# First 1024 tokens' attention by pairs of heads instead of by 128 tokens, in an attention and two-MLP kernel on one core

## The chip, the cores and the metric

The kernel runs on one core of a Trainium2 chip. The metric is the device time of one execution in microseconds (us); lower is better. Engines are named as in the profile: PE (matrix products), PEld (its loads of the stationary operand), DVE (vector), ACT (scalar), POOL, and SP, which issues the DMAs.

## The reference

Chunked attention, then two gated MLPs over the same 4608 tokens (8 batches of 576 tokens, 8 heads of 64).

```python
B, H, S, D = 8, 8, 576, 64                  # q, k, v
q_c, k_c, v_c = (t.reshape(B, H, 9, 64, D) for t in (q, k, v))
scores = matmul(q_c, k_c^T) / sqrt(D)       # 64 x 64 in each chunk
attn = softmax(scores)
x = matmul(attn, v_c)                       # to [4608 tokens, 512]
g = x @ w_gate                              # 512 -> 1536
x = (g * sigmoid(g) * (x @ w_val)) @ w_out  # 1536 -> 512
xn = x / sqrt(mean(x*x) + 1e-6) * rms_g
out = the same gated MLP on xn with the second set of weights
```

The MLP weights arrive as 64-bit floats; the kernel loads them as pairs of 32-bit words and makes a high and a low part of each on the chip.

## The kernel before, in words

The tokens are cut into 9 blocks of 512 (j), a block into 4 tiles of 128 tokens (i = 0 to 35; a tile is two chunks). The hidden width is cut into 12 pieces of 128 (f). The first MLP runs per block j and piece f: `emit_g` (12 products: 4 pieces of the contraction, each as high x high, low x high, high x low), `emit_v` (12 more), and `emit_y` of the piece before (12). `mm3` issues the three products (L493 to L495). The second MLP follows, with a seven-product scheme that the change does not touch.

The order of all instructions is written out by hand. The table `at` holds small steps (attention of the next block, loads, weight preparation) that run at set places between `emit_g`, `emit_v` and `emit_y`; `put(l, j, pos, fn)` enters one, and three positions make one f.

Ahead of the loop stands a start written out step by step, the attention of tiles 0 to 3, that is of the first block. Per tile:

- `load_tok` (L305): q and k of 128 tokens and all 8 heads, one DMA each, in pieces of 64 floats;
- `trans_tok` (L312, copies L321): 4 + 4 PE transposes of 128 x 128, one per pair of heads, and two ACT copies into `qT`, `kT`;
- `att_s` (L355): 16 score products of 64 x 64;
- `att_m` (L374, L375, L381): maximum and subtraction on DVE, exponential on ACT;
- `att_n` (L388 to L393): sum and reciprocal on DVE, product on POOL;
- `att_t` (L417, L424): 4 PE transposes and a copy to `pT`;
- `att_pv` (L451): 16 products with `xv`; the cast of the result to `xh` on ACT (L469) and the rest, `xl`, on DVE (L487, `att_lo`).

Tiles 4 to 7 (the second block) take the same steps from the table, between the products of block 0. Tiles from 8 on use `trans_att` and `att_both`, and are left alone.

The first MLP's weights are prepared in the list order `w1` = g0, v0, o0, g1, v1, o1, ... (piece number behind the letter), three DVE and three ACT operations each: `rebase` (ACT L112, L116), `to_f32` (DVE L131, L136), the cast to the high part (ACT L152), `to_lo` (DVE L159). `conv1(z)` does one step of that for three weights at once; `pre_w1` issues their loads (512 KB each, L101).

PSUM has the pairs of banks `a` and `yb` (two banks each) and the banks `g`, `v`, `y0`, `y1`.

Of the kernel before, what the change touches and what calls it, by code (L numbers as in the profile page):

```python
# [9 lines left out]
F32 = mybir.dt.float32  # L10
# [9 lines left out]
def tile_kernel(  # L20
# [192 lines left out]
    groups = [list(range(0, 2 * EARLY - 2)), list(range(2 * EARLY - 2, 2 * EARLY))]  # L213
# [37 lines left out]
    def load_v(g):  # L251
        if g == 0:
            two = [spare_tile([P, 2, HP, D], f"xv_0_{n}") for n in range(len(groups[0]) // 2)]
            gt.setdefault(g, [None] * 3)[2] = lambda z, hp, n, hpar: two[n // 2][z:z + 64, hpar, hp, :]
            dmas = []
            for n, t in enumerate(two):
                s = n * P
                for hpar, z, c, w in ((0, 0, 0, P), (1, 64, 0, CH), (1, 0, CH, CH)):
                    dmas.append((
                        t[z:z + w, hpar],  # L260
                        v[0, hpar::2, s + c:s + c + w, :].rearrange("h p d -> p h d"),
                    ))
            return dmas
# [21 lines left out]

    def load_tok(i):
        ts_ = []
        dmas = []
        for nm, src in (("q", q), ("k", k)):
            if i < EARLY:  # L290
                t = spare_tile([P, H, D], f"t{nm}{i}")
            else:
                z, f = again.pop(0)
                t = wraw.tile([P, H, D], F32, tag=f"w{z}{f}", name=f"t{nm}{i}")
# [6 lines left out]
    def trans_tok(i, tags=None):  # L301
        ts_ = []
        both = ps_pair("a", f"qkP{i}") if tags is None else None
        pts = []
        for z, nm in enumerate("qk"):  # L305
            t = tok[i][z]
            if both is None:
                pt = ps.tile([P, HP, P], F32, tag=tags[z], name=f"{nm}P{i}")
            else:
                pt = both[:, z].rearrange("p (h q) -> p h q", h=HP)  # L310
# [4 lines left out]
            pts.append(pt)  # L315
        for z, nm in enumerate("qk"):
            if i < NW // P:
                sb = spare_tile([P, HP, P], f"{nm}T{i}")
            else:
                sb = att.tile([P, HP, P], F32, tag=f"{nm}T", name=f"{nm}T{i}")  # L320
            nc.scalar.copy(sb, pts[z])  # L321
            ts_.append([sb[:, hp] for hp in range(HP)])
        qkT[i] = ts_
# [23 lines left out]
    def att_s(i, tag="a", sb=None):  # L347
        qT, kT = qkT.pop(i)
        if sb is None:
            sb = ps_pair(tag, f"s_{i}")[:, :, :HP * CH]  # L350
# [89 lines left out]
    def att_pv(i, j, tag="a", xb=None, put_off=False):  # L440
        pT = probT.pop(i)
        if xb is None:
            xb = ps_pair(tag, f"xb_{i}")[:, :, :HP * CH]
        xb = xb.rearrange("p c (h q) -> p c h q", h=HP)
        for hp in range(HP):
            for c in range(2):
                g, n = where[2 * i + c]
                vt = gt[g][2]
                for hpar in range(2):
                    z = (hpar ^ c) * 64  # L450
                    nc.tensor.matmul(  # L451
                        xb[hpar * 64:hpar * 64 + 64, c, hp, :],
                        vt(z, hp, n, hpar),
                        pT[z:z + 64, hp, c * 64:c * 64 + 64],
                        start=True,
                        stop=True,
                    )
        xh, xl = x_tiles(0, j)
        o = i * P - blocks[j][0]
# [4 lines left out]

    def att_hi(i, j):
        xb = xps[i]
        xh, xl = x_tiles(0, j)
        o = i * P - blocks[j][0]
        nc.scalar.copy(xh[:, :, o:o + P].rearrange("p h (c q) -> p c h q", c=2), xb)  # L469
# [12 lines left out]
    def att_lo(i, j):  # L482
        xb = xps.pop(i)
        xh, xl = x_tiles(0, j)
        o = i * P - blocks[j][0]
        ah, al = (t[:, :, o:o + P].rearrange("p h (c q) -> p c h q", c=2) for t in (xh, xl))
# [9 lines left out]

    def emit_g(l, j, f):
# [3 lines left out]
        g = ps.tile([P, 512], F32, tag="g", name=f"g{l}_{j}_{f}")  # L501
        for c in range(KD):
# [157 lines left out]
    for x, (l, j) in enumerate(seq):  # L660
        if x + 1 < len(seq):
            nl, nj = seq[x + 1]
            if nl == 0:
                for n, i in enumerate(tiles_of(nj)):
# [13 lines left out]
                    else:  # L678
                        b = (0, 9, 18, 27)[n]
                        late = n == 0  # L680
                        put(l, j, b + (2, 1, 0, 0)[n], lambda i=i: trans_tok(i))
                        put(l, j, b + 2 + late, lambda i=i: att_s(i))
# [5 lines left out]
                    for c in (2 * i, 2 * i + 1):  # L688
                        g = where[c][0]
                        if g > 0 and c == groups[g][-1] and g + 2 < len(groups):  # L690
                            dq, dv, nq = {4: (21, 18, 10), 7: (3, 9, 12), 8: (8, 12, 12)}.get(i, (1, 11, 8))
# [14 lines left out]
    spread(0, 0, 4, 10, lambda: load_v(2))  # L706
# [298 lines left out]
    with tc.manual_schedule():  # L1005
        nc.vector.memset(ones.bitcast(F32), 1.0)
        make_identity(nc, ident)
        w1 = [(nm, f) for f in range(NF) for nm in "gvo"]
        loaded = 0
# [33 lines left out]

        NI = NW // P
        issue(load_tok(0))
        issue(load_tok(1))
        issue(load_tok(2))
        issue(load_tok(3))
        first_v = load_v(0)
        issue(first_v[:3])  # L1050
        pre_w1(1)
        issue(first_v[3:])
# [3 lines left out]
        later = load_v(1)  # L1056
        sb_ = ("a", "yb")
        xb_ = (("g", "v"), ("y0", "y1"))
        trans_tok(0, xb_[0])
        trans_tok(1, xb_[1])  # L1060
        att_s(0, sb_[0])
        att_m(0)
        trans_tok(2, xb_[0])
        att_s(1, sb_[1])
        att_m(1)
        trans_tok(3, xb_[1])
        att_n(0)
        att_s(2, sb_[0])
        att_m(2)
        att_n(1)  # L1070
        att_s(3, sb_[1])
        att_t(0, xb_[0][0])
        rebase(0, *w1[0])
        att_m(3)
        att_n(2)
        att_t(1, xb_[1][0])
        att_n(3)
        att_pv(0, 0, "a")
        att_pv(1, 0, "yb")
        att_lo(0, 0)  # L1080
        att_lo(1, 0)
        att_t(2, xb_[0][1])
        att_t(3, xb_[1][1])
        to_f32(0, *w1[0], cast=False)
        att_pv(2, 0, "a")
        cast_hi(*w1[0])
        att_pv(3, 0, "yb")
        att_lo(2, 0)
        to_lo(*w1[0])
        att_lo(3, 0)  # L1090
        rebase(0, *w1[1])
        conv1(1)
# [188 lines left out]
```

## Time and profile before

| | us |
|---|---|
| median of 3 runs (1751.49 to 1754.25) | 1751.93 |
| profiled execution, its own time | 1752.0 |
| its span | 1750.2 |
| PE busy (10086 matmuls) | 1732.6, 99% of the span |
| DVE busy | 1262.3, 72% |
| ACT busy | 674.4, 39% |
| POOL busy | 393.4, 22% |
| DMA: 379.73 MB, mean | 217 GB/s |

Busy time is the union of an engine's instructions. "Idle before" names what ended an engine's wait. In lists in order of time a group of equal instructions is one line with its count. A product of full 32-bit floats (scores, and the products with `xv`) is recorded as two matmuls, so 16 score products show as x32; a transpose, and a product of the MLP, is recorded as one. Matmuls overlap, so the time from one start to the next is what one costs, and the duration beside it is longer.

### The profile page before, as it was taken

The numbers are of one execution on the slowest core, as the hardware profiler recorded it, in microseconds if no ns is written. First come the engines' busy times: TensorE is split into PE (matmuls) and PEld (weight loads), VectorE is DVE, ScalarE is ACT, GpSimd is POOL, SyncE is SP. The second block draws the span as 40 slices with busy tenths as digits, with TensorE's granted clock in tenths as the row PEclk, the third lists the DMA queues.
The fourth block names the chain that finished last, engine by engine and source line by source line (L and its number), as shares of the span: only waits on it lengthen the run. The fifth ranks groups of instructions, "written<-read, shape, count | busy, mean of one in ns | idle before, by whom it ended". The sixth has DMA issues, their size and how long they took to land.

```text
span 1750.2 us, 28897 instructions
## 1 busy us (share of the span) xinstructions
PE 1732.6 (99%) x10086; PEld 1468.3 (84%) x10086; DVE 1262.3 (72%) x2250; ACT 674.4 (39%) x1248; POOL 393.4 (22%) x391
## 2 busy tenths in 40 slices
PE   7999999999999999999999999999999999999998
PEld 5788888888888888888888888888888888999998
DVE  6986887888878788876536567944794488568566
ACT  6872333233332422332122434523453354345343
POOL 1002244244423524341121211200110011002000
PEclk9999999999999999999999999999999999999999
DMA  9997777876877776763435576787678768988986
GB/s 235 319 266 200 205 220 225 231 199 193 243 215 208 222 239 174 222 208 115 144 97 192 167 237 195 210 250 217 192 206 254 213 176 240 298 268 261 293 253 174
DMA packets 451393, 379.73 MB, mean 217 GB/s; under 512 B 275632, under 2 KB 302256, under 8 KB 451248
## 3 DMA queue, kind: packets, MB, share of 16 engines
q1 hardware_dynamic: 449648, 377.68, 73.4%
q8 instruction: 81, 1.33, 0.3%
q14 instruction: 64, 0.52, 0.1%
q10 hardware_dynamic: 1600, 0.20, 0.1%
HBM read 316.41 MB, written 61.34 MB: 216 GB/s over the span
## 4 chain that ended last, share of the span: by engine, by line
PE 96%; DVE 2%; issue 1%; ACT 1%; DMA 0%; SPq 0%; POOL 0%; POOLq 0%; DVEq 0%; ACTq 0%
PE g L493 6%; PE g L494 6%; PE g L495 6%; PE v L493 5%; PE v L494 5%; PE v L495 5%; PE y L493 3%; PE y L495 3%; PE y L494 3%; PE y_b L495 3%; PE y_b L493 3%; PE y_b L494 3%; PE ygA L494 1%; PE ygA L495 1%; PE ygA L493 1%; PE yvA L493 1%
## 5 line engine op out<-in xcount | busy, mean ns | idle before, releaser
L493 PE MATMUL g<-xh,wg 128*128 128x512 f32 x432 | 169.0, 391 | 1.8 <-ACT xh L469 1.1
L493 PE MATMUL v<-xh,wv 128*128 128x512 f32 x432 | 169.1, 391 | 0.7 <-ACT wo L152 0.7
L494 PE MATMUL g<-xl,wg 128*128 128x512 f32 x432 | 168.3, 390 | 0.4 <-DVE xl L487 0.4
L495 PE MATMUL g<-xh,lg 128*128 128x512 f32 x432 | 168.4, 390 | 0.0
L495 PE MATMUL v<-xh,lv 128*128 128x512 f32 x432 | 168.3, 389 | 0.0
L494 PE MATMUL v<-xl,wv 128*128 128x512 f32 x432 | 168.2, 389 | 0.0
L525 ACT CAST hh<-sg 128x512 fp32r<-128x512 f32 x108 | 67.2, 622 | 240.0 <-DVE sg L522 239.9
L892 POOL TENSOR_TENSOR h<-h,h 128x512 f32<-128x512 f32 (+1 forms) x30 | 37.1, 1236 | 518.9 <-DVE h L870 518.9
L505 ACT ACTIVATE sg<-g 128x512 f32<-128x512 f32 x108 | 64.5, 597 | 204.2 <-PE g L495 203.7
L409 DVE STREAM_TRANSPOSE pT<-p 32x128 f32<-32x128 f32 x448 | 135.5, 302 | 7.2 <-POOL p L393 0.9
L506 DVE SCALAR_TENSOR_TENSOR sg<-sg,g 128x512 f32<-128x512 f32 x108 | 73.1, 676 | 85.9 <-ACT sg L505 85.6
L928 DVE TENSOR_TENSOR hl<-h,hh 128x512 fp32r<-128x512 f32 (+1 forms) x180 | 121.5, 704 | 6.0 <-ACT hh L927 5.9
L927 ACT CAST hh<-h 128x512 fp32r<-128x512 f32 (+1 forms) x180 | 100.4, 577 | 46.9 <-PE yvA L495 20.4
L851 DVE TENSOR_TENSOR sgt<-sgt,sig 128x512 f32<-128x512 f32 (+1 forms) x90 | 58.3, 648 | 74.3 <-ACT sig L850 74.3
L850 ACT ACTIVATE sig<-sgt 128x512 f32<-128x512 f32 (+1 forms) x90 | 53.2, 591 | 144.8 <-DVE sgt L858 144.8
L393 POOL TENSOR_TENSOR p<-p,r 128x512 f32<-128x512 f32 x36 | 39.3, 1091 | 282.2 <-DVE r L392 268.0
L527 DVE TENSOR_TENSOR hl<-sg,hh 128x512 fp32r<-128x512 f32 x108 | 86.7, 803 | 20.0 <-ACT hh L525 19.9
L522 DVE SCALAR_TENSOR_TENSOR sg<-v,sg 128x512 f32<-128x512 f32 x108 | 74.1, 686 | 37.5 <-PE v L495 36.0
L493 PEld LDWEIGHTS g<-xh,wg 128*128 128x128 f32 x432 | 81.1, 188 | 19.2 <-ACT xh L469 1.3
L493 PEld LDWEIGHTS v<-xh,wv 128*128 128x128 f32 x432 | 81.1, 188 | 18.4 <-ACT wo L152 1.1
L494 PEld LDWEIGHTS g<-xl,wg 128*128 128x128 f32 x432 | 81.1, 188 | 17.5 <-DVE xl L487 0.7
L495 PEld LDWEIGHTS g<-xh,lg 128*128 128x128 f32 x432 | 81.1, 188 | 17.4 <-DVE lg L159 0.4
(806 smaller groups left out, 4699.8 us busy)
## 6 DMA issues: line engine op xcount, KB each, us to landing
wrg<-w_scratch SPq DMA_DIRECT2D x210, 256.0 KB, 3.2
wrv<-w_scratch SPq DMA_DIRECT2D x210, 256.0 KB, 3.4
wro<-w_scratch SPq DMA_DIRECT2D x210, 256.0 KB, 3.1
lg<-lo_scratch SPq DMA_DIRECT2D x96, 256.0 KB, 2.9
lv<-lo_scratch SPq DMA_DIRECT2D x96, 256.0 KB, 3.3
lo<-lo_scratch SPq DMA_DIRECT2D x96, 256.0 KB, 3.9
w_scratch<-wsg SPq DMA_DIRECT2D x42, 256.0 KB, 2.8
w_scratch<-wsv SPq DMA_DIRECT2D x42, 256.0 KB, 2.5
```

The source lines that it names most:

```text
L409: nc.vector.transpose(out=pT[o:o + 32, :, r:r + 32], in_=pt[r:r + 32, :, z, b * 32:b * 32 + 32])
L493: nc.tensor.matmul(o, sh, mh, start=first, stop=False, skip_group_check=free)
L494: nc.tensor.matmul(o, sh, ml, start=False, stop=False, skip_group_check=free)
L495: nc.tensor.matmul(o, sl, mh, start=False, stop=last, skip_group_check=free)
L505: nc.scalar.activation(sg[:, :n], g[:, :n], AF.Tanh, scale=0.5)
L506: return sg, lambda: nc.vector.scalar_tensor_tensor(out=sg[:, :n], in0=sg[:, :n], scalar=1.0, in1=g[:, :n], op0=ALU.add, op1=ALU.mult)
L522: nc.vector.scalar_tensor_tensor(out=sg[:, :n], in0=vv[:, :n], scalar=0.5, in1=sg[:, :n], op0=ALU.mult, op1=ALU.mult)
L525: nc.scalar.copy(hh[:, :n], sg[:, :n])
L527: return product, lambda: nc.vector.tensor_sub(hl[:, :n], sg[:, :n], hh[:, :n].bitcast(F32))
L851: nc.vector.tensor_mul(t[:, :tw], src[:, :tw], sg[:, :tw])
L927: nc.scalar.copy(hh[:, :tw], src)
L928: nc.vector.tensor_sub(hl[:, :tw], src, hh[:, :tw].bitcast(F32))
```

## The change

The attention of the first 1024 tokens (two blocks) is cut otherwise: a step i now is one pair of heads over 512 tokens, not 128 tokens over all heads. i = 0 to 3 are the four pairs of block 0, i = 4 to 7 those of block 1.

- `load_tok` lays 4 consecutive tokens of a head side by side on a partition, so that a piece is 256 floats (1024 bytes). `load_vp` brings v of a pair, still in pieces of 64 floats. The weight g0 is loaded ahead of pair 3.
- `trans_half` replaces the transposes: for q, then for k, 8 plain products with the identity, each 64 columns of tokens' data (one head) against 128, into one half of the output's partitions. The ACT copy behind it puts the tokens back in order.
- `spin` issues products of `ones` with itself, whose result nobody reads: 12 at the beginning, and 6, 4 and 4 in the start.
- The scores and the products with v of two pairs share one pair of PSUM banks (`quad`).
- A pair's result is one of the four pieces of the first MLP's contraction. `part_g` issues the 12 products of the first `emit_g` (block 0, piece 0) one by one, as soon as their pair and weight part are there; `emit_g` then skips them.
- In the order of weights, g1 changes places with o0.
- Tiles 4 to 7 keep their places in the table. Groups of chunks for the later tiles begin at chunk 16; before, a group held chunks 15, 16, 17.

The core of the diff:

```diff
     def load_tok(i):
+        base, h0 = i // HP * NW, 2 * (i % HP)
...
-            for o, n, b, p in chunks_of(i * P, P):
-                dmas.append((t[o:o + n], src[b, :, p:p + n, :].rearrange("h t d -> t h d")))
+            for o, n, b, p in pieces(base, NW):
+                dmas.append((
+                    t[o // 4:(o + n) // 4],
+                    src[b, h0:h0 + 2, p:p + n, :].rearrange("h (p e) d -> p h e d", e=4),
+                ))
...
-            for hp in range(HP):
-                nc.tensor.transpose(
-                    pt[:, hp, :], t[:, 2 * hp:2 * hp + 2, :].rearrange("p a b -> p (a b)"), ident
+    def trans_half(i, z, pt):
+        nm = "qk"[z]
+        for e in range(4):
+            for h in range(2):
+                nc.tensor.matmul(
+                    pt[64 * h:64 * h + 64, e * P:(e + 1) * P], tok[i][z][:, h, e, :], ident,
+                    start=True, stop=True,
                 )
...
+        nc.scalar.copy(
+            sb.rearrange("p a b -> p (a b)").rearrange("p (t e) -> p t e", e=4),
+            pt.rearrange("p (e t) -> p t e", e=4),
+        )
+        qkT.setdefault(i, []).append([sb[:, c] for c in range(HP)])
...
+    def spin(n, tag):
...
+        for _ in range(n):
+            nc.tensor.matmul(t[:, :P], ones, ones, start=True, stop=True)
...
+    def x_part(i, j):
+        if i < 2 * HP:
+            return [t[:, i % HP].rearrange("p (h c q) -> p c h q", c=2, q=CH) for t in x_tiles(0, j)]
...
+    def part_g(z, c):
+        if not first:
+            first.append(ps.tile([P, 512], F32, tag="g", name="g0_0_0"))
+        xh, xl = x_tiles(0, 0)
+        r = whi[0, "g", 0].rearrange("p (c f) -> p c f", c=KD)
+        if z == 2:
+            r = wl_[0, 0, 0, "g"].rearrange("p (c f) -> p c f", c=KD)
+        nc.tensor.matmul(
+            first[0], r[:, c], (xh, xl, xh)[z][:, c], start=(z, c) == (0, 0), stop=(z, c) == (1, KD - 1)
+        )
...
-        for c in range(KD):
+        for c in range(KD if (l, j, f) != (0, 0, 0) else 0):
...
         w1 = [(nm, f) for f in range(NF) for nm in "gvo"]
+        w1[2:4] = w1[3], w1[2]
...
+        spin(12, "a")
+        quad = [ps_pair(tag, f"quad{tag}") for tag in ("a", "yb")]
+        quad = [t[:, :, z:z + HP * CH] for t in quad for z in (0, HP * CH)]
...
+        turn(0, 0, "g")
+        turn(0, 1, "v")
+        turn(1, 0, "y0")
+        att_s(0, quad[0])
+        turn(1, 1, "y1")
+        turn(2, 0, "g")
         att_m(0)
...
+        att_s(1, quad[1])
```

What the program's order of PE says. At the very start (qP, kP: q and k turned, in PSUM; s or quad: scores), before:

```order
L312 MATMUL qP_155<-ident,tq_103 128x128 x4
L312 MATMUL kP_160<-ident,tk_104 128x128 x4
L312 MATMUL qP_169<-ident,tq_107 128x128 x4
L312 MATMUL kP_174<-ident,tk_108 128x128 x4
L355 MATMUL s_183<-kT_167,qT_165 64x64 x16
L312 MATMUL qP_205<-ident,tq_111 128x128 x4
L312 MATMUL kP_210<-ident,tk_112 128x128 x4
L355 MATMUL s_219<-kT_181,qT_179 64x64 x16
```

and with the change:

```order
L376 MATMUL spin_155<-ones 128x128 x12
L349 MATMUL qP_170<-ident,tq_103 64x128 x8
L349 MATMUL kP_181<-ident,tk_104 64x128 x8
L349 MATMUL qP_192<-ident,tq_107 64x128 x8
L408 MATMUL quada<-kT_190,qT_179 64x64 x16
L349 MATMUL kP_219<-ident,tk_108 64x128 x8
L349 MATMUL qP_230<-ident,tq_111 64x128 x8
L408 MATMUL quada<-kT_228,qT_201 64x64 x16
```

The first scores now stand behind 24 products of 64 x 128 instead of 16 transposes of 128 x 128, the second behind 40 instead of 24.

Where the first block's attention ends and the first gate begins, before (tp: probabilities turned; xb: product with v):

```order
L417 MATMUL tp_377<-ident,p_278 128x128 x4
L417 MATMUL tp_384<-ident,p_316 128x128 x4
L451 MATMUL xb_394<-pT_382,xv_2_121 64x64 x16
L451 MATMUL xb_413<-pT_389,xv_3_122 64x64 x16
L493 MATMUL g_0_0_459<-xh_0_354,wg_0_393 128x512
L494 MATMUL g_0_0_459<-xl_0_355,wg_0_393 128x512
L495 MATMUL g_0_0_459<-xh_0_354,lg_0_0_432 128x512
```

and with the change:

```order
L558 MATMUL g_0_0_405<-xh_0_381,lg_0_0_472 128x512 x2
L470 MATMUL tp_476<-ident,p_396 128x128 x4
L558 MATMUL g_0_0_405<-xh_0_381,wg_0_386 128x512
L558 MATMUL g_0_0_405<-xh_0_381,lg_0_0_472 128x512
L558 MATMUL g_0_0_405<-xl_0_382,wg_0_386 128x512
L504 MATMUL quadyb<-pT_481,xv_132 64x64 x16
L558 MATMUL g_0_0_405<-xh_0_381,wg_0_386 128x512
L558 MATMUL g_0_0_405<-xh_0_381,lg_0_0_472 128x512
L558 MATMUL g_0_0_405<-xl_0_382,wg_0_386 128x512
L545 MATMUL v_0_0_544<-xh_0_381,wv_0_510 128x512
```

Behind the last pair's products with v, 3 products of the first gate are left, where there were 12.

In the loop, step 5, between `emit_v` and `emit_y`, before:

```order
L495 MATMUL v_0_3_828<-xh_0_354,lv_0_3_741 128x512
L312 MATMUL qkP_844<-ident,tq_455 128x128 x4
L312 MATMUL qkP_844<-ident,tk_456 128x128 x4
L493 MATMUL y_0_0_643<-hh_0_2_725,wo_0_637 128x512
L494 MATMUL y_0_0_643<-hl_0_2_726,wo_0_637 128x512
```

and with the change:

```order
L546 MATMUL v_0_3_896<-xl_0_382,wv_0_775 128x512
L547 MATMUL v_0_3_896<-xh_0_381,lv_0_3_809 128x512
L349 MATMUL qkP_912<-ident,tq_526 64x128 x8
L349 MATMUL qkP_912<-ident,tk_527 64x128 x8
L545 MATMUL y_0_0_709<-hh_0_2_793,wo_0_703 128x512
```

The place is the same; 8 transposes have become 16 plain products.

## Rows read from the trace of the kernel before

**Rows 1.** The page's first part: busy time of each engine (share, instructions).

```profile
span 1750.2 us, 28897 instructions
PE 1732.6 (99%) x10086; PEld 1468.3 (84%) x10086; DVE 1262.3 (72%) x2250; ACT 674.4 (39%) x1248; POOL 393.4 (22%) x391
```

**Rows 2.** Busy time by stretch: length, PE, PEld, DVE, ACT, POOL, PE clock, DMA, GB/s.

```profile
9.90:26.40 16.50, 11.71 (x258) 9.30 (x258) 14.09 (x27) 11.61 (x21) 4.17 (x4) 0.90 1.00 246
26.40:51.20 24.80, 22.69 (x129) 17.20 (x129) 22.95 (x38) 19.57 (x36) 1.32 (x1) 1.00 1.06 282
51.20:60.00 8.80, 8.66 (x66) 6.89 (x67) 8.80 (x15) 8.25 (x16) 0.00 (x0) 1.00 0.92 249
60.00:80.00 20.00, 20.00 (x153) 16.22 (x152) 19.90 (x34) 16.03 (x30) 1.33 (x1) 1.00 1.08 336
110.00:1740.00 1630.00, 1629.55 (x9219) 1386.25 (x9218) 1166.14 (x2087) 591.40 (x1102) 384.60 (x378) 1.00 0.72 214
```

**Rows 3.** PE in order of time: start, duration, what [idle before].

```profile
4.17 1.09 PE L312 MATMUL qP<-ident,tq 128*128 128x128 f32 x4 [4.17 <-DMA tq<-in_q_dram]
...
8.71 1.13 PE L355 MATMUL s<-kT,qT 64*64 64x64 f32 x32
9.78 1.11 PE L312 MATMUL qP<-ident,tq 128*128 128x128 f32 x4
...
12.40 0.66 PE L312 MATMUL qP<-ident,tq 128*128 128x128 f32 x4
...
29.01 0.39 PE L493 MATMUL v<-xh,wv 128*128 128x512 f32 x1
29.24 0.39 PE L494 MATMUL v<-xl,wv 128*128 128x512 f32 x1
...
51.16 0.50 PE L494 MATMUL y<-hl,wo 128*128 128x512 f32 x1 [0.49 <-DVE hl L527]
...
60.31 0.60 PE L312 MATMUL qkP<-ident,tq 128*128 128x128 f32 x4
60.74 0.60 PE L312 MATMUL qkP<-ident,tk 128*128 128x128 f32 x4
61.10 0.48 PE L493 MATMUL y<-hh,wo 128*128 128x512 f32 x1
...
64.01 0.69 PE L355 MATMUL s<-kT,qT 64*64 64x64 f32 x32
64.63 0.50 PE L493 MATMUL g<-xh,wg 128*128 128x512 f32 x1
```

**Rows 4.** DVE in order of time, same columns.

```profile
9.91 0.69 DVE L374 TENSOR_REDUCE m<-s 128x8 f32<-128x512 f32 x1 [8.92 <-PE s L355]
...
12.54 0.69 DVE L374 TENSOR_REDUCE m<-s 128x8 f32<-128x512 f32 x1 [1.21 <-PE s L355]
...
17.22 0.64 DVE L374 TENSOR_REDUCE m<-s 128x8 f32<-128x512 f32 x1
...
28.67 0.69 DVE L159 TENSOR_TENSOR lv<-crv,wv 128x512 fp32r<-128x512 f32 x1
...
50.42 0.68 DVE L527 TENSOR_TENSOR hl<-sg,hh 128x512 fp32r<-128x512 f32 x1
```

**Rows 5.** DMA from 5 to 10 us: packets, bytes, rate, packets under a size.

```profile
DMA packets 4346, 1.10 MB, mean 219 GB/s; under 512 B 4346, under 2 KB 4346, under 8 KB 4346
```

**Rows 6.** DMA from 20 to 25 us.

```profile
DMA packets 1254, 1.65 MB, mean 330 GB/s; under 512 B 43, under 2 KB 1125, under 8 KB 1253
```

**Rows 7.** ACT in order of time.

```profile
6.41 0.58 ACT L321 COPY kT<-kP 128x512 f32<-128x512 f32 x1 [0.53 <-PE kP L312]
...
20.63 0.58 ACT L469 CAST xh<-xb 128x512 fp32r<-128x512 f32 x1 [0.51 <-PE xb L451]
```

**Rows 8.** PE alone in two stretches: length, busy, clock, DMA, GB/s.

```profile
4.00:8.70 4.70, 4.35 (x16) 1.00 1.33 221
...
19.40:21.30 1.90, 1.90 (x65) 0.50 0.81 185
```

**Rows 9.** DVE after the first scores: xl and its waits for the cast.

```profile
21.25 0.69 DVE L487 TENSOR_TENSOR xl<-xb,xh 128x512 fp32r<-128x512 f32 x1 [0.18 <-ACT xh L469]
```

More of the change, by code (lines that the diff above doesn't have):

```diff
@@ L284, in tile_kernel, with pieces, load_vp @@
     again = [(nm, f) for f in (NF - 2, NF - 1) for nm in "gvo"]
+    def pieces(n0, n):
+        t = n0
+        while t < n0 + n:
+            b, p = divmod(t, S)
+            m = min(n0 + n - t, S - p)
+            yield t - n0, m, b, p
+            t += m
+    vp = {}
+    def load_vp(i):
+        base, h0 = i // HP * NW, 2 * (i % HP)
+        if i < HP:
+            t = spare_tile([P, 2, HP, D], f"xv{i}")
+        else:
+            if i % 2 == 0:
+                vp["both"] = ax.tile([P, HP, 5, D], F32, tag="xv", name=f"xv{i}")
+            t = vp["both"].rearrange("p a b d -> p (a b) d")[:, 8 * (i % 2):8 * (i % 2) + 8]
+            t = t.rearrange("p (z c) d -> p z c d", z=2)
+        vp[i] = t
+        dmas = []
+        if base + NW <= S:
+            src = v[0, h0, base:base + NW, :].rearrange("(c p) d -> p c d", p=P)
+            dmas.append((t[:, 0], src))
+            src = v[0, h0 + 1, base:base + NW, :].rearrange("(c z p) d -> z p c d", z=2, p=CH)
+            dmas += [(t[64 - 64 * z:128 - 64 * z, 1], src[z]) for z in range(2)]
+            return dmas
+        for hpar in range(2):
+            for z in range(2):
+                run = []
+                for c in range(HP):
+                    b, p = divmod(base + (2 * c + z) * CH, S)
+                    if run and run[-1][1] == b:
+                        run[-1][3] += 1
+                    else:
+                        run.append([c, b, p, 1])
+                o = 64 * (hpar ^ z)
+                for c, b, p, m in run:
+                    for cc in range(m if p + 2 * CH * m > S else 1):
+                        if p + 2 * CH * m > S:
+                            a = p + 2 * CH * cc
+                            dmas.append((
+                                t[o:o + 64, hpar, c + cc], v[b, h0 + hpar, a:a + CH, :],
+                            ))
+                        else:
+                            src = v[b, h0 + hpar, p:p + 2 * CH * m, :].rearrange(
+                                "(c z p) d -> z p c d", z=2, p=CH
+                            )
+                            dmas.append((t[o:o + 64, hpar, c:c + m], src[0]))
+        return dmas
     def load_tok(i):
+        base, h0 = i // HP * NW, 2 * (i % HP)
         ts_ = []
@@ L299, in load_tok, with trans_tok @@
         return dmas
[L301 to L310, printed above, removed]
-            for hp in range(HP):
-                nc.tensor.transpose(
-                    pt[:, hp, :], t[:, 2 * hp:2 * hp + 2, :].rearrange("p a b -> p (a b)"), ident
-                )
[L315 to L323, printed above, removed]
+    def trans_half(i, z, pt):
[5 more added lines that the diff above has]
+                    start=True, stop=True,
+                )
+        if i < HP:
+            sb = spare_tile([P, HP, P], f"{nm}T{i}")
+        else:
+            sb = att.tile([P, HP, P], F32, tag=f"{nm}T", name=f"{nm}T{i}")
+        nc.scalar.copy(
[3 more added lines that the diff above has]
+        qkT.setdefault(i, []).append([sb[:, c] for c in range(HP)])
+    def trans_tok(i):
+        both = ps_pair("a", f"qkP{i}")
+        for z in range(2):
+            trans_half(i, z, both[:, z])
+    spun = []
+    def spin(n, tag):
+        t = ps_pair(tag, f"spin{len(spun)}")[:, 0] if tag == "a" else ps.tile(
+            [P, 512], F32, tag=tag, name=f"spin{len(spun)}"
+        )
+        spun.append(t)
+        for _ in range(n):
+            nc.tensor.matmul(t[:, :P], ones, ones, start=True, stop=True)
     def issue(dmas):
@@ L457, in att_pv @@
                     )
-        xh, xl = x_tiles(0, j)
-        o = i * P - blocks[j][0]
         xps[i] = xb
@@ L1042, in conv1 @@
                 keep.pop(0)
[L1044 to L1047, printed above, removed]
+        for i in range(3):
+            issue(load_tok(i))
+        pre_w1(1)
         issue(load_tok(3))
[L1049 to L1052, printed above, removed]
+        issue(load_vp(0) + load_vp(1))
+        pre_w1(2)
+        issue(load_vp(2) + load_vp(3))
         pre_w1(5)
```

127 lines of the change are left out of this document (67 added, 60 removed).

## The prediction

> **What bounds the kernel now.** I read the page first, then the busy time by stretch, then PE, DVE and ACT in order of time, last the DMA. PE is busy for 1732.6 of 1750.2 us [rows 1], so 17.6 us are idle. 4.17 of them lie ahead of its first product, which waits for the first q [rows 3]. From 51.2 us on there is hardly any: 8.66 of 8.80, 20.00 of 20.00 and 1629.55 of 1630 us are busy [rows 2]. The last wait that counts is at 51.16, for DVE's `hl` of f = 1 [rows 3]. So two prices decide. Work that PE gains or loses behind 51 us shows in full. Ahead of 51 us only the time counts at which that `hl` is ready.
>
> That time is DVE's. From 9.9 to 26.4 us it is busy for 14.09 of 16.50, from 26.4 to 51.2 for 22.95 of 24.80 [rows 2]. It starts at 9.91 behind the first scores and makes `hl` at 50.42 [rows 4]. In the program's order 64 operations stand from the first maximum to this `hl`, before and after, and the last of them is the same; inside, the preparation of g0 moves ahead and g1 changes places with o0. PE could be done earlier and would wait.
>
> **The loads.** A tile's q or k is 0.262 MB. In pieces of 256 bytes the DMAs moved 219 GB/s [rows 5], so 1.2 us each; where most packets were larger they moved 330 [rows 6], so 0.8 us. The first q landed at 4.17 and should land 0.4 earlier, at 3.7, the others at 4.5, 5.3, 6.1, 6.9 and 7.7; then the weight (0.52 MB, 1.6 us) at 9.3, and the last q and k at 10.1 and 10.9. The fourth pair is needed at about 11 and later, so the weight ahead of it costs nothing; without that slack it would cost up to 1.6. SP issues v and five weights behind this; g1's weight lands some 3 us before ACT reaches it, which covers SP's waits.
>
> **What one half costs.** PE turned q and k of a tile in 0.79 us (60.31 to 61.10) [rows 3], 8 transposes. Now it takes 16 plain products, 32 matmuls in the profile's count, of 128 columns on half the array's columns. No row shows such a product. From below: as cheap as the transposes, 0.79. From above: 32 matmuls, each like a transpose of 128 columns with nothing beside it, 0.43 / 4 = 0.107 us, in all 3.4. The nearest row is that of the scores, also plain 32-bit, 32 matmuls of 64 columns on a quarter of the array: 0.62 us warm (64.01 to 64.63) and 1.07 early (8.71 to 9.78) [rows 3]. The difference says that about 0.45 of the 0.62 goes with the clock. Twice the columns on twice the area is four times that, 1.8, plus the 0.17 that stays: 1.97. Twice the columns alone is 1.24. I take 1.75, nearer the upper one, so 0.87 for one half (q or k), and 1.7 while the clock is at its lower level.
>
> **The start.** PE's transposes last 1.1 us for four until 9.78 and 0.66 from 12.40 on [rows 3]: the lower of the two levels, 1.2 against 2.4 GHz, although the clock's column reads 1.00 there [rows 8]. Before the rise PE had done transposes, and from 8.71 scores. The change puts 12 plain products at about 1.05, behind the memset, so I let the higher level begin at 5.0; if it begins at 8, all of this comes 1.7 later.
> - q of pair 0 from 3.7: 1.3 us at the lower level do three quarters, done at 5.2. Then k to 6.1 and q of pair 1 to 6.95, which the order puts ahead of the scores. The copy of k (0.58) [rows 7] is done at 6.9. Scores to 7.6; DVE starts at 7.75 instead of 9.91.
> - Behind the scores: 0.87 for k of pair 1, 0.87 for q of pair 2. The second scores also wait for DVE's subtraction of pair 0 (the two share PSUM banks), done at 9.1, and run from 9.4 to 10.0. DVE's second maximum is at 10.15 instead of 12.54, so 2.4 us earlier.
> - Then new waits take some back. `xl` of pair 0 now waits for the cast of pair 1, not its own, which stands behind pair 1's products and an exponential: about 1.0. `xl` of pair 2 comes behind a loop through three engines: `xl` of pair 1, a gate product that waits for it (0.23, from 29.01 to 29.24 [rows 3]), pair 2's products with v (0.62, like the scores), a cast (0.58), two handovers (0.13 each, as from 9.78 to 9.91), less DVE's `lg` in between (0.65): about 1.1. The third, for pair 3: 0.4. Together 2.5. Before, the same stretch had 16.50 - 14.09 = 2.4 idle, of which 1.21 were the wait for the second scores [rows 2, 4] and 1.2 others like that of [rows 9]. The chain so gives back 1.3 of the 2.4, and about 1.0 is left.
>
> From `lv` at 28.67 to `hl` at 50.42 [rows 4] the work on DVE is the same, 33 operations, so the 1.0 stays. The first gate's products between the pairs give PE time (its 9 early products, 2 us) where DVE sets the end: nothing in the sum. The spins between the pairs stand where PE waits anyway; they replace the drop of the clock to 0.50 at 19.4 to 21.3 [rows 8], worth some 0.6 us on PE, and DVE then waited only 0.18 for it [rows 9]: nothing, too. If DVE were not the limit, both would count, 2 to 3 us. Bounds for the start: a gain of 3.6 if no new wait bites, a loss of 0.6 if the clock rises late.
>
> **The loop.** Steps 4 to 7 keep their places. Step 4 (0.95 more on PE) lies ahead of 51 us, where PE has about 1 us to spare beside DVE: hidden, and up to 0.95 if not. Steps 5 to 7 lie where PE never waits: 3 x (1.75 - 0.79) = 2.9 us in full; by the bounds 0 to 7.8. The copies behind them take as many elements as before, and ACT's cast with a strided pattern takes 0.58 like the plain copy [rows 7], so their patterns cost nothing. Longer turns give DVE and ACT more time, not less. The loads of steps 4 to 7 come in larger pieces and hold no one up.
>
> **Sum.** 1752.0 (the profiled execution; its span is 1750.2, the median of the runs 1751.93) - 1.0 + 2.9 = 1753.9; say 1754.0. About 0.2%, 3.5 us, is what a measurement of this kernel can tell from no change, so the forecast lies within it.
>
> **The rivals.**
> - *Cheap products, start passed on whole (faster).* If the halves run side by side so well that a tile costs what its transposes did, the loop loses nothing, and a half at 0.43 lets DVE start at 6.5 and reach the second maximum at 8.65: 3.9 earlier. With the new waits 2.7 are left, 1749.3; if they don't bite, 3.9, 1748.1. For it: the scores' quarters do run side by side (0.62 for 32 matmuls is 0.019 each). Against: it needs twice the gain that this row shows, and the waits stand in the order. It decides the sign only below 0.9 a tile.
> - *The halves don't run side by side (slower).* At 3.4 a tile, or 1.7 a half, PE becomes the limit of the start: scores of pair 0 at 10.1, of pair 3 at 20.9, so DVE's fourth maximum comes at 21.0 instead of 17.22 [rows 4]; with g0's preparation, two operations of 0.69, already done, that is 2.4 late. With 7.8 in the loop: 1762. From 2.3 a tile on the change is slower by more than 3.5. For it: all 128 rows are in use, and no row shows two column halves at once. Against: the scores' row. On the page "TensorE: Matmul & The Clock Gate" (Terms) the Trainium skill says that the transpose mode is 4 times faster for 32-bit floats; by that a tile costs 4 x 0.79 = 3.2, and the sum is 1752.0 + 7.2 - 1.0 = 1758.2. On its page "TensorEngine Tiling (Array Packing)" (Theoretical Speedup) it allows twice the speed where one dimension is 64; by that 3.4 becomes 1.7, and the sum stays at 1753.8. No row shows either for this shape.
> - *The start is not earlier.* The spins could hold PE: at the early transposes' 0.275 each, 12 take 3.3 us from 1.05, to 4.35, and the first q waits 0.65; with a clock that rises late the gain is gone: 1752.0 + 2.9 = 1754.9.
>
> **How the numbers follow.** Forecast 0.62, cheap products 0.18, not side by side 0.15, no earlier start 0.05. The forecast's own range is 1750.5 to 1757.0: a tile of 1.24 to 2.4 (1.4 to 4.8 in the loop) and a start between a gain of 2.5 and none. The range, 1748.5 to 1759.0, takes that in, most of the first rival and the lower part of the second. Faster by over 0.2%: nearly all of the cheap case, 0.17. Slower by over 0.2%: 0.15, plus a sixth of the forecast (tiles above 2.3, or no gain at the start), 0.12 with the last rival's share: 0.27. Within: 0.56.
>
> **What would show it.** In the profile after: the first q's product at 3.7; q and k of step 5 in 1.75 us from the first of 32 matmuls to the next product (0.8 or 3.4 for the rivals); DVE's first maximum at 7.75 and second at 10.15; waits of DVE for casts on `xl` of some 1.0 and 1.1; `hl` of f = 1 at 49.4; no PE wait behind 52 us. I am wrong if step 5 takes under 1.0 or above 2.3, if PE waits behind 52 us, or if PE's clock falls again between 10 and 30 us.

## The result, and the profile after

The changed kernel takes 1762.08 us (median, 1761.11 to 1765.64); the kernel before took 1751.83 on the same chip. The ratio is 1.0059, 95% interval 1.0042 to 1.0077: slower by about 10 us, 8 more than forecast and above the range. The profiled execution took 1761.65 us, its span is 1759.9.

The page's first part of the kernel after answers to [rows 1]. PE is busy 12.5 us longer.

```profile
span 1759.9 us, 29343 instructions
PE 1745.1 (99%) x10304; PEld 1479.2 (84%) x10304; DVE 1264.5 (72%) x2250; ACT 675.0 (38%) x1248; POOL 394.2 (22%) x391
```

Busy time by stretch of the kernel after, columns as in [rows 2]. PE, which had no idle time between 60 and 80 us, now has 0.68 there. The stretch from 38.80 is the second gate; its clock is 0.62, and no such stretch stood there before.

```profile
9.90:26.40 16.50, 14.84 (x307) 12.03 (x304) 13.90 (x26) 11.15 (x20) 4.46 (x4) 1.00 1.00 248
26.40:38.80 12.40, 8.07 (x85) 5.20 (x83) 10.87 (x18) 9.51 (x17) 0.00 (x0) 1.00 0.88 246
38.80:43.30 4.50, 4.50 (x14) 3.31 (x12) 2.64 (x5) 4.00 (x7) 0.00 (x0) 0.62 0.99 297
...
60.00:80.00 20.00, 19.32 (x137) 15.45 (x136) 16.88 (x29) 13.22 (x25) 1.33 (x1) 1.00 0.83 253
```

PE of the kernel after in order of time, as in [rows 3]. `qkP` with `tq` are q's products of a step, with `tk` k's. Step 4 is at 33.54, step 5 at 64.54.

```profile
3.80 1.98 PE L349 MATMUL qP<-ident,tq 128*64 128x128 f32 x16
...
8.93 0.69 PE L408 MATMUL quada<-kT,qT 64*64 64x64 f32 x32
...
30.24 0.50 PE L545 MATMUL v<-xh,wv 128*128 128x512 f32 x1 [0.41 <-ACT wv L152]
...
33.54 1.09 PE L349 MATMUL qkP<-ident,tq 128*64 128x128 f32 x16
37.77 1.09 PE L349 MATMUL qkP<-ident,tk 128*64 128x128 f32 x16 [3.14 <-ACT qT L357]
38.80 0.50 PE L545 MATMUL g<-xh,wg 128*128 128x512 f32 x1
...
43.33 0.69 PE L408 MATMUL s<-kT,qT 64*64 64x64 f32 x32
...
64.54 1.09 PE L349 MATMUL qkP<-ident,tq 128*64 128x128 f32 x16
66.32 1.09 PE L349 MATMUL qkP<-ident,tk 128*64 128x128 f32 x16 [0.68 <-ACT qT L357]
67.35 0.50 PE L545 MATMUL y<-hh,wo 128*128 128x512 f32 x1
...
150.86 0.69 PE L408 MATMUL both<-kT,qT 64*64 64x64 f32 x32
```

PE of the kernel before at the same places: step 4's turn, the next gate, and the last scores that are issued in block 0 (of a later tile, named `both`).

```profile
31.84 0.60 PE L312 MATMUL qkP<-ident,tq 128*128 128x128 f32 x4
32.27 0.60 PE L312 MATMUL qkP<-ident,tk 128*128 128x128 f32 x4
33.56 0.50 PE L493 MATMUL g<-xh,wg 128*128 128x512 f32 x1 [0.69 <-ACT wg L152]
...
37.11 0.69 PE L355 MATMUL s<-kT,qT 64*64 64x64 f32 x32 [0.24 <-ACT kT L321]
...
140.31 0.69 PE L355 MATMUL both<-kT,qT 64*64 64x64 f32 x32
```

Two brackets of the kernel after tell the story: k's products wait for ACT's copy of q. The view of PE's waits (engine, tile and line, what it waited for: us in total, times, longest) adds them up over the whole kernel after:

```profile
PE qkP L349 <- ACT qT L357: 5.2, 4, 3.1
```

ACT of the kernel after, around step 4, shows why the first of them is the long one: q's products end at 34.6, but ACT does its queue in order, and the copy starts at 37.14, behind casts that wait for DVE.

```profile
36.02 0.62 ACT L152 CAST wv<-crv 128x512 fp32r<-128x512 f32 x1 [0.23 <-DVE crv L136]
36.62 0.62 ACT L590 CAST hh<-sg 128x512 fp32r<-128x512 f32 x1
37.14 0.58 ACT L357 COPY qT<-qkP 128x512 f32<-128x512 f32 x1
38.92 0.59 ACT L357 COPY kT<-qkP 128x512 f32<-128x512 f32 x1 [1.19 <-PE qkP L349]
```

DVE of the kernel after answers to [rows 4] and [rows 9]: first two maxima a little earlier, the fourth 1.9 later, `hl` of f = 1 at 52.87 for 50.42.

```profile
9.69 0.69 DVE L427 TENSOR_REDUCE m<-quada 128x8 f32<-128x512 f32 x1 [8.69 <-PE quada L408]
...
12.21 0.69 DVE L427 TENSOR_REDUCE m<-quada 128x8 f32<-128x512 f32 x1 [1.10 <-PE quada L408]
...
17.79 1.42 DVE L136 SCALAR_TENSOR_TENSOR crg<-crg,cmg 128x512 uint32<-128x512 uint32 x1
19.13 0.68 DVE L427 TENSOR_REDUCE m<-quadyb 128x8 f32<-128x512 f32 x1
...
21.85 0.69 DVE L539 TENSOR_TENSOR xl<-quada,xh 128x512 fp32r<-128x512 f32 x1 [0.28 <-ACT xh L523]
...
24.05 1.26 DVE L159 TENSOR_TENSOR lg<-crg,wg 128x512 fp32r<-128x512 f32 x1
26.01 0.69 DVE L539 TENSOR_TENSOR xl<-quadyb,xh 128x512 fp32r<-128x512 f32 x1 [0.70 <-ACT xh L523]
28.59 0.69 DVE L539 TENSOR_TENSOR xl<-quadyb,xh 128x512 fp32r<-128x512 f32 x1 [0.57 <-ACT xh L523]
...
40.66 0.69 DVE L131 SCALAR_TENSOR_TENSOR cmg<-stage,cmg 128x512 uint32<-128x512 uint32 x1 [2.28 <-ACT cmg L116]
...
52.87 0.68 DVE L592 TENSOR_TENSOR hl<-sg,hh 128x512 fp32r<-128x512 f32 x1
```

Beside the trace of before, the lateness grows in three places. The first product of v is 1.23 late (30.24 for 29.01). Behind step 4's turn the next gate is 5.24 late (38.80 for 33.56) and takes 4.53 to the scores behind it for 3.55. After that PE is behind DVE: it waits no more for `hl` or for other work of DVE and ACT, and by 58.25, where step 4's products with v begin, 4.15 are left (54.10 before). Then each of the steps 5 to 7 adds 2.0: a turn lasts 2.81 (64.54 to 67.35) where it lasted 0.79 (60.31 to 61.10). Where the last scores issued in this block start, PE is 10.55 late (150.86 for 140.31), and the whole span is 9.7 longer.

### The profile page after: what moved, and what is told of

Its sections match the earlier page's. It is cut to its first block, busy times and chain, and to the rows that moved or that the text cites. A ratio compares the mean times of both kernels' runs of the same rounds, so it can differ in the third digit from the quotient of the medians.

```text
span 1759.9 us, 29343 instructions
## 1 busy us (share of the span) xinstructions
PE 1745.1 (99%) x10304; PEld 1479.2 (84%) x10304; DVE 1264.5 (72%) x2250; ACT 675.0 (38%) x1248; POOL 394.2 (22%) x391
## 4 chain that ended last, share of the span: by engine, by line
PE 96%; DMA 1%; DVE 1%; ACT 1%; SPq 1%; issue 0%; POOL 0%; ACTq 0%; POOLq 0%
PE g L545 6%; PE v L545 6%; PE g L547 6%; PE g L546 6%; PE v L547 6%; PE v L546 6%; PE y L545 3%; PE y L547 3%; PE y L546 3%; PE y_b L547 3%; PE y_b L546 3%; PE y_b L545 3%; PE ygA L546 1%; PE yvA L547 1%; PE ygA L547 1%; PE yvA L546 1%
## 5 line engine op out<-in xcount | busy, mean ns | idle before, releaser
L547 PEld LDWEIGHTS v<-xh,lv 128*128 128x128 f32 x432 | 81.1, 188 | 17.4 <-DVE lv L159 0.5
```

The costliest lines, as they stand in the source:

```text
L547: nc.tensor.matmul(o, sl, mh, start=False, stop=last, skip_group_check=free)
```

## The experiments

The theory after this reading: most of the loss is the wait of k's products for the copy of q. Both write one tile of two PSUM banks, and the copy is issued between them. The rest is the price of the products in the loop and something at the start. The rival: the products' price and the start are the whole loss.

**1. Both products ahead of both copies.** One function changes:

```diff
-        for z in range(2):
-            trans_half(i, z, both[:, z])
+        for part in range(2):          # 0: products alone, 1: copies alone
+            for z in range(2):
+                trans_half(i, z, both[:, z], part)
```

> Base: the changed kernel; in steps 4 to 7 the products of q and of k are issued both before the two ACT copies, as the transposes were before; nothing else. Theory A (the loss is mostly PE's wait of k's products for ACT's copy of q, which share a pair of PSUM banks): the turn of steps 5 to 7 falls from 2.81 to about 1.9 us each (-2.7 in all), the wait of 3.14 and the low clock (0.62) behind step 4 go, first gate product of piece 1 at about 35.4 instead of 38.80; time about 1757. Theory B (the loss is the price of the plain products): the wait only moves, less than 1 us faster, 1761 to 1762. Theory C (the late start is what lasts): less than 2.7 us faster, since step 4 then waits for DVE instead.

1755.80 us, ratio 1.0018 (1.0009 to 1.0028): 6.3 us come back. PE of this version in order of time, the gate behind step 4, step 5, and the last scores; no wait is left behind 30 us on line 349.

```profile
36.03 0.50 PE L548 MATMUL g<-xh,wg 128*128 128x512 f32 x1
...
62.19 1.09 PE L349 MATMUL qkP<-ident,tq 128*64 128x128 f32 x16
63.12 1.04 PE L349 MATMUL qkP<-ident,tk 128*64 128x128 f32 x16
64.09 0.50 PE L548 MATMUL y<-hh,wo 128*128 128x512 f32 x1
...
145.79 0.69 PE L411 MATMUL both<-kT,qT 64*64 64x64 f32 x32
```

A turn now takes 1.90 (62.19 to 64.09): the price of the products by themselves. In step 4 the next gate starts at 36.03 instead of 38.80, and its granted clock is 1.00. The theory stands. One thing in this trace is not the edit's work: up to step 4 the instructions are those of the changed kernel, and yet the first product of v comes 0.58 later (30.82 for 30.24; 31.04 in version 2), since PE stood idle 0.87 ahead of k's products of pair 3 where it stood 0.19 (1.01 in version 2). The profile names no other engine and no DMA for it, and in version 4 there is no such pause; its cause stays open. So a single trace places the first product of v to no better than about 0.8 us.

**2. The same, and the second block turned by transposes.** The pairs stay; q and k are loaded with the two heads side by side, in pieces of 256 bytes and one DMA for each head. The edit for steps 4 to 7, shortened:

```diff
-        for e in range(4):
-            for h in range(2):
-                nc.tensor.matmul(pt[64 * h:64 * h + 64, e * P:(e + 1) * P], tok[i][z][:, h, e, :], ident, ...
+        for e in range(4):
+            nc.tensor.transpose(pt[:, e * P:(e + 1) * P], turned[:, e * P:(e + 1) * P], ident)
```

> Base: e1; in steps 4 to 7 q and k are turned by 4 + 4 transposes of 128 x 128 instead of 16 plain products (their loads put the 4 tokens of a head apart, in pieces of 64 floats). Price of the products: a turn of 1.85 against 0.8 us, so 3 x 1.05 = 3.2 us below e1, and nothing more from step 4 if DVE sets that end: about 1754. If plain products were no dearer than the transposes: the same time as e1.

A turn costs 0.79 again, and behind step 7 PE is 3.4 us ahead of version 1 (v at 115.49 for 118.92). But the time is 1757.85, ratio 1.0032 (1.0022 to 1.0041; runs from 1753.70 to 1761.32), not better. DVE of this version shows where the gain went: it waits for buffers of the weights' low parts, whose writes to memory are late, and PE then waits 2.2 for `wo`.

```profile
128.24 0.69 DVE L159 TENSOR_TENSOR lg<-crg,wg 128x512 fp32r<-128x512 f32 x1 [3.36 <-DMA lo_scratch<-lg]
...
133.81 0.69 DVE L159 TENSOR_TENSOR lv<-crv,wv 128x512 fp32r<-128x512 f32 x1 [2.07 <-DMA lo_scratch<-lv]
```

The longest such wait was 0.8 before and 1.6 in version 1. What makes the writes late (more issues on SP, or smaller pieces) was not separated.

**3. Transposes at the start too**, with loads in 256-byte pieces there.

> Base: e2; the start (steps 0 to 3) also turns by transposes. If the plain products make the start late (at the lower clock 1.7 us for a half, against 1.1 for four transposes): scores of pair 0 at about 7.4 instead of 8.93, first product of emit_v 1 to 2 us earlier than in e2, time 1752 to 1753. If they pay for themselves by raising the clock earlier: the clock rises later than at 8.9, and the first product of emit_v is not earlier or later than in e2.

1761.87, ratio 1.0052 (1.0037 to 1.0067). From 5 to 10 us the DMAs move 195 GB/s in this version and 316 in the changed kernel; the first q's transposes start at 5.08, and the first product of v at 33.07; PE alone waits 2.55 for the fourth pair's q. So the transposes were not had in pairs for nothing: in this layout they need the small pieces, in twice as many DMAs, and which of the two costs more was not separated.

**4. Version 1 without the first 12 spinning products** (the line `spin(12, "a")` left out).

> Base: e1; the 12 spins at the beginning are left out. If they bring the clock's rise forward: matmuls at the higher level only from 10 us or later instead of 8.9, scores and all behind them 1 us or more later. If the rise hangs on the products from 3.8 on alone: the first q's products at 3.7, the rise at 8.9 as before, scores within 0.2 us of e1's.

A single execution: 1755.77. q's products start at 3.69, the first three halves take 1.73, 1.71 and 1.70, the fourth 0.93, and the scores between them start at 8.83; with the spins it was 8.82 in version 1 and 8.93 in the changed kernel. The 12 products did nothing that shows for the clock.

**5. Version 1 with the first gate in one piece** behind the last pair, instead of woven between the pairs.

> The version with both turns ahead of both copies, but the first gate's 12 products stand in one piece behind the start's attention, as before, instead of between the pairs. Theory (the start is paced by the chain VectorE - GpSimd - TensorE - ScalarE of the four pairs, not by TensorE's own work): the first three quarters of the gate do not need the last pair, so they run while the last part of x is made; the first product of v (30.8 us there) moves by no more than 0.5 either way, 1755.3 to 1756.5. Rival (weaving is worth the nine products that it puts into gaps, 9 x 0.23 = 2.1 us): v at 32.9, 1757.9.

Not settled. The first product of v comes at 30.86, for 30.82 woven, as the theory said, but the woven starts have it anywhere from 30.07 (version 4) to 31.04 (version 2). The time, 1757.34, ratio 1.0029 (1.0018 to 1.0040), lies 0.8 above the theory's range and 0.6 below the rival's 1757.9; its interval and version 1's overlap. The trace has a second lesson. In this execution the clock rose at 5.6 already and DVE's first maximum came at 8.28, 1.3 earlier than with the late rise. DVE kept that lead to the fourth maximum (17.73 for 19.03 in version 1). Then, without woven products, PE waited, its clock was 0.50 from 23 to 27 us, and the gate took 4.2. At the first product of v nothing of the early start was left.

**6. The calls of the start in the order of before**: rounding behind the fourth maximum, gate in one piece, no spins; pairs and their PSUM tiles as in the change.

```diff
-        rebase(0, *w1[0])
         att_s(2, quad[2])
...
+        att_t(0, "g")
+        rebase(0, *w1[0])
+        att_m(3)
```

> The version with both turns ahead of both copies and without the first 12 spinning products; the start keeps the pairs, the 1024-byte loads and the products by the identity, but its calls stand in the order of before: the weights' rounding behind the fourth pair's maximum, no spinning products, the gate in one piece. Theory (the start loses because 2.0 us of the weights' work stand ahead of the fourth pair's maximum and because each low part then waits for a cast that stands behind other work): fourth maximum back at 17 to 17.6 us from 19.0, last low part at 26 to 27 from 28.4, first product of v at 29 to 29.7 from 30.1, 1754.8 to 1755.5. Rival (the products by the identity and the clock's rise set the start): v at 30.1 or later, 1755.8 or more.

Not what the theory said: 1758.47, ratio 1.0038 (1.0023 to 1.0053), the first product of v at 33.62. DVE of this version says why:

```profile
24.12 1.29 DVE L542 TENSOR_TENSOR xl<-quada,xh 128x512 fp32r<-128x512 f32 x2 [2.05 <-ACT xh L526]
...
28.41 0.69 DVE L542 TENSOR_TENSOR xl<-quadyb,xh 128x512 fp32r<-128x512 f32 x1 [1.67 <-ACT xh L526]
```

In the change two pairs' scores, and later their x, share one tile of two banks (`quada`, `quadyb`). In the old order pair 1's products with v wait for the cast of pair 0 and both `xl` for both casts; PE waited, and its clock was 0.50 from 20 to 26 us. So this version does not tell what the order costs: in the old order the shared tile costs far more (version 9 keeps the order without the shared tile: 28.61).

**7 and 8. The two halves of the change apart.** Version 7 has the new start (without the first spins) and the second 512 tokens as before; version 8 the old start and the second 512 tokens in pairs, with both products ahead of both copies.

```diff
     def load_tok(i):
+        if i >= HP:                 # version 7; version 8: if i < HP
+            return load_tok_t(i)    # by 128 tokens, as before
```

> The new start in pairs (without the first 12 spinning products), but the second 512 tokens as before: loads by 128 tokens, transposes, values by chunks. Theory (of the 3.5 us that are left, the start costs what the first product of v is late, 1.06, and the turns of the second block the rest): 1753.0 to 1753.9, turns of steps 5 to 7 0.79 again, second block's distances as before. Rival (most of what is left was lost at the start, and shows later only): 1755 or more.

> The start of before (by 128 tokens) and the second 512 tokens in pairs with both turns ahead of both copies. Theory: first product of v at 29.0 as before, four turns at 1.9 for 0.79 add up to 4.4 us less what an idle TensorE covers, 1754.3 to 1756; with the kernel that has only the new start the two differences from before add up to about 3.5. Rival (the second block in pairs costs nothing once the wait is gone): 1752.7 or less.

Version 7: 1753.17, ratio 1.0009 (0.9999 to 1.0018), 1.1 above the 1752.06 of before; the interval just takes in no difference. Its first product of v comes at 30.10, 1.09 late, and it is 1.08 late at 141.39, where the last scores of this block start. Version 8: 1755.04, ratio 1.0017 (1.0008 to 1.0027), 3.0 above. Together 4.1, for 3.5 expected. PE of version 7, then of version 8:

```profile
30.10 0.51 PE L582 MATMUL v<-xh,wv 128*128 128x512 f32 x1 [0.39 <-ACT wv L152]
...
141.39 0.69 PE L445 MATMUL both<-kT,qT 64*64 64x64 f32 x32
```

```profile
143.66 0.69 PE L463 MATMUL both<-kT,qT 64*64 64x64 f32 x32
```

In version 8 the product that waits for `hl` of f = 1 is not late, although step 4's turn is 1.1 longer: that one is hidden. The other three are not: 3.35 late at the last scores (143.66 for 140.31), although its first product of v came 0.35 early (28.66).

**9. Only the pairs' loads and products at the start.** Order, PSUM tiles and second block as before.

```diff
-        quad = [ps_pair(tag, f"quad{tag}") for tag in ("a", "yb")]
-        quad = [t[:, :, z:z + HP * CH] for t in quad for z in (0, HP * CH)]
+        quad = ("a", "yb", "a", "yb")     # a pair of banks for one pair of heads at a time
```

> Only the start's pairs, 1024-byte loads and products by the identity; everything else as before: order of the calls, one pair of PSUM banks for one pair of heads at a time, order of the weights, second 512 tokens by transposes. Theory (the start in old order with two pairs of heads in one pair of banks lost by the waits for the other's readers, 0.94 to 2.05 us each on VectorE, and by the low clock that followed; and the start of before is paced by VectorE from its first maximum to lv): without the shared banks VectorE's chain runs as before from a first maximum at 9.6 to 9.8, lv at 28.4 to 28.7, first product of v at 28.7 to 29.1, 1751.6 to 1752.4, no difference from before. Rival (the products by the identity are what the start loses): first product of v at 30 or later, 1753 or more.

1751.95 against 1752.33, ratio 1.0001 (0.9991 to 1.0010): no difference, as the theory said. DVE starts at 9.01, 0.9 earlier than before, and `lv` is at 28.59, 0.08 earlier. The lead is gone at the third maximum: in this order its scores stand behind pair 3's products, and DVE waits. DVE of before, then of this version:

```profile
14.91 0.64 DVE L374 TENSOR_REDUCE m<-s 128x8 f32<-128x512 f32 x1
```

```profile
14.92 0.69 DVE L464 TENSOR_REDUCE m<-s 128x8 f32<-128x512 f32 x1 [0.94 <-PE s L445]
```

PE of this version at the first product of v, which waits for ACT:

```profile
28.61 0.50 PE L582 MATMUL v<-xh,wv 128*128 128x512 f32 x1 [0.34 <-ACT wv L152]
```

So the 1024-byte pieces and the products by the identity, taken together, cost this start nothing, nor do they bring it more than 0.4 us: what the loads give, the dearer products take back.

**10. Version 7 with the first weights' rounding behind the fourth maximum.**

```diff
-        to_f32(0, *w1[0])
         att_t(1, "y0")
         att_m(3)
+        to_f32(0, *w1[0])
```

> The kernel with the new start and the old second block, with one thing changed: the first weights' rounding on VectorE stands behind the fourth pair's maximum instead of ahead of it. Theory (2.0 us of it, 0.7 of that from standing beside GpSimd's product, hold the fourth pair up): fourth maximum at 17.0 to 17.6 instead of 19.0, last low part 0.5 to 1.5 earlier, first product of v at 28.9 to 29.8 instead of 30.1, 1752.0 to 1753.0. Rival (the waits for the casts come first, the rounding only fills): first product of v within 0.3 of 30.1, 1753.2.

Not better, and in the trace worse, which neither theory expected: 1754.44, ratio 1.0013 (1.0003 to 1.0022), first product of v at 31.98 for version 7's 30.10. The two intervals overlap. The fourth maximum does come at 16.77. But the first woven product needs `wg`, whose cast is now later; PE waits 1.31 for it with everything else behind, and `xl` of pair 0 is at 22.25 for 21.71. The weaving is what ties PE to the rounding. That is 0.5 of the 1.9; the rest comes later, where the granted clock was 0.50 from 25.0 to 28.3 (1.00 in version 7).

**11. Version 9 with 16 spinning products in PE's gaps.**

> The version with only the pairs in the old frame, with 6, 6 and 4 spinning products in the gaps of TensorE between 16 and 24 us. Theory (VectorE and ScalarE pace the start down to wv and lv, so a higher clock there frees TensorE only): granted clock 0.95 or more from 16 to 28 us, first gate 2.8 to 3.0 us instead of 3.2 to 3.5, first product of v no more than 0.4 earlier than without the spins, 1751.2 to 1752.4. Rival (the low clock of 16 to 26 us costs the start what it costs TensorE, over 1 us): 1750.9 or less.

The granted clock is 1.00 in every stretch from 16 to 30 us, but in the profiled execution of version 9 it was that without the spins, so this tells little of the clock. They bring nothing: 1753.16, ratio 1.0007 (0.9997 to 1.0017), first product of v at 29.21, 0.6 later. The gate is as long as in version 9 (3.73 to the next product, for 3.72), and not the 2.8 to 3.0 that was expected: in both it starts behind ACT's `wg`, and the next product waits for ACT's `wv` (0.36 and 0.34).

**12. Version 7 with one pair of banks for one pair of heads**, by the same edit as in 9; order, weaving and spins stay.

> The kernel with the new start and the old second block, its order, weaving and spinning products kept, but one pair of PSUM banks for one pair of heads at a time instead of two pairs of heads in one. Theory (the 1.1 us that this start loses are the waits in the shared banks): the two waits of 0.70 of the values' products for the cast of another pair's x are gone, the first product of v comes at 28.6 to 29.5 instead of 30.1, 1751.9 to 1752.7. Rival (the start loses by its order: the rounding of the first weights ahead of the fourth pair's maximum, the woven products in TensorE's queue): first product of v within 0.4 of 30.1, 1753.0 or more.

1752.06 against 1752.44, ratio 0.9998 (0.9988 to 1.0007): no loss is left that can be measured, and the first product of v is at 29.39. But the expectation named the wrong waits. The two of 0.70 on PE are still there: they are the woven gate's own wait for the cast of x. What went is the one that the prediction had named, `xl` of pair 0 behind the cast of pair 1. DVE of version 7, then of version 12; up to there its operations start within 0.02 us of each other in the two:

```profile
21.71 0.69 DVE L576 TENSOR_TENSOR xl<-quada,xh 128x512 fp32r<-128x512 f32 x1 [0.60 <-ACT xh L560]
```

```profile
21.02 0.64 DVE L576 TENSOR_TENSOR xl<-xb,xh 128x512 fp32r<-128x512 f32 x1
```

These 0.69 are the 0.71 by which v starts earlier. The other 0.78 to version 9 are what is left for the order, rounding and weaving; this is by subtraction, and no version takes it apart.

## Why the prediction was wrong

By parts, in us: the wait for the copy of q 6.3 (the changed kernel less version 1), the second block's products 3.0 (version 8), the new start 1.1 (version 7, whose interval takes in no difference). Together 10.4, for 10.25 measured. The prediction had 0, 2.9 and -1.0. It had priced 1762 for a rival, halves that do not run side by side; that the time came out there is chance, for that rival's turn of 3.4 us did not come.

- **The step that failed: a wait was missing.** The prediction gave step 4 as "hidden" and the other turns as two halves of 0.87 with nothing between. In the changed program q's copy is issued between q's and k's products, and k's products wait for it because they go to the same tile. Before, all eight transposes were issued ahead of both copies, which also read that tile, so no such wait could arise. In steps 5 to 7 it is a copy and two handovers, 0.68 of idle time and 0.9 on the turn (2.81 for 1.90 in version 1); in step 4 it is ACT's whole queue, 3.14. A late gate and a clock of 0.62 followed, and DVE, which had paced this part, waited 2.28 itself. PE's wait behind 52 us and step 5's turn above 2.3 were two of the prediction's own signs of being wrong. That the copies last no longer for their new pattern (0.58) was right; when they are issued was not asked.
- **The products' price was right**: 1.75 forecast, 1.90 measured, so 1.1 more than the transposes for each turn. Both named rivals on it fall: 0.79 and 3.4. By the Trainium skill ("Perfetto Trace Analysis", Optimizing Tensor Performance) a logical transpose should be done as a transpose and not as a standard matmul; the trace agrees, 0.44 against 0.93 a half. From 1.97 as an upper guess it was taken down to 1.75 without a row; the row's own scaling was nearer. The factor of 4 by which the prediction's text made 3.2 a tile did not come in this shape: 1.90 for 0.79 is 2.4. Step 4's turn was hidden, as said, once the wait was gone (version 8).
- **The first loads were right**: first q ready at 3.69 (version 4) for 3.7, 316 GB/s for 330.
- **The clock of the start was wrong.** It was taken to rise at 5.0 and rose at 8.9, so DVE began at 9.69 and not 7.75. The prediction had priced this: a loss of 0.6 in place of a gain of 1.0. The measured loss is 1.1 to 1.2. What an early rise would have brought is seen only in version 5, whose DVE was 1.3 ahead down to the fourth maximum.
- **The new waits of the start were of the right kind.** `xl` of pair 0, expected 1.0, cost 0.7 (version 12; its bracket is 0.28 in the changed kernel and 0.60 in version 7); those of pairs 2 and 3, 1.1 and 0.4, show as 0.70 and 0.57. Missing was that `crg` and `lg`, set beside POOL's products by the new order, take 1.42 and 1.26 us for 0.69.
- **The bound of the start was half right.** From DVE's third maximum to `lv` the chain is as long as before (13.67 us in version 9 for 13.76). Ahead of it PE has a say: in the old order a start of DVE 0.9 earlier is lost in the wait of 0.94 for scores that stand behind pair 3's products (version 9). In the change's order that wait is absent, but the rounding stands ahead of the fourth maximum instead.

The medians give 6.3 for the wait, the spans of the two profiled executions 5.1. Version 1's trace had the start that was 0.58 late with the same instructions; from the first product of v to the last scores the two traces differ by 5.65 (120.62 for 114.97). The 0.6 that is left is within the spread of the runs of one kernel, 1.5 to 7.6 us here.

No version tried is faster than the kernel before by more than can be measured; versions 9 and 12 equal it.

## What to carry to other kernels

When a change rewrites a producer and its reader as one helper called twice, look at what is now issued between the two producers: a tile of PSUM that both write makes the second producer wait for the first one's reader, and the wait is as long as that reader's queue (here 0.7 us in three places and 3.1 in one). An engine that is never idle hides nothing, so a wait of 0.7 us repeated there is paid each time. And when a start comes earlier, follow it to the next place where an engine waits: here 0.9 us was gone at the third maximum.

## What the runs showed of the hardware that was not expected

- **The clock at the start does not show in its column.** The granted clock reads 1.00 from 0 to 14 us in all these traces, while one half takes 1.7 us in the first microseconds and 0.93 later. By these durations the rise came 3.4 to 5.3 us after the first product by the identity (at 7.3 in version 9, 8.9 in the changed kernel), and once 1.8 after it (version 5, whose instructions are the same up to there as in version 1, at 8.8). With transposes first it came later: at about 11.7 before and 10.9 in version 8. Spinning products from 1.05 to 3.80 made no visible difference. What decides this was not found.
- **The clock fell behind a pause, not in it.** PE had no product in flight from 34.7 to 37.7 in step 4; the granted clock read 1.00 there and up to 38.8, then 0.50 from 39.4 to 42.7, with PE busy without a gap. The gate took 4.53, where version 1, with no pause, took 2.95.
- **DVE beside POOL (GpSimd).** `crg<-crg,cmg` and `lg<-crg,wg` took 1.42 and 1.26 us where POOL's product `p<-p,r` ran (1.33 for 1.04 in one case), and 0.69 where it did not; DVE's subtraction `p<-quadyb,m`, one of whose inputs is in PSUM, kept 0.69 beside it. By the Trainium skill ("SBUF — State Buffer", SBUF: two separate sides) a VectorE operation with two SBUF inputs and a GpSimd operation that reads SBUF exclude each other; the trace agrees.
